# Third and fourth x chunks loaded by one transposing DMA, and the final wait moved from SyncE to ScalarE

## The chip, the core and the metric

The kernel runs on one core of a Trainium2 chip. The metric is the time of one execution on the device in microseconds (us); lower is better. A profile is one further execution, recorded by the hardware profiler; it gives a span (first to last instruction of the program) and a record of every instruction, DMA packet and semaphore update.

The core's engines are named PE (TensorE, matmuls), DVE (VectorE), ACT (ScalarE), POOL (GpSimd) and SP (SyncE). SP computes nothing here: its program issues nearly all DMAs and waits for what they need.

## The reference

Two blocks read the same x (2048 tokens, width 512) and are mixed by a gate for each token:

```python
x = A_x
g = _sigmoid((x * gate_w).sum(-1, keepdims=True))
a = _A_ref(x, A_wqkv, A_w_phi, A_wo)   # linear attention, 32 heads of 16:
                                       # softmax feature maps of +-q and +-k, kv sums, o = num / den, o @ wo
b = _B_ref(x, B_w1, B_w2)              # relu(x @ w1) @ w2, inner width 1376
return g * a + (1 - g) * b
```

All inputs and the output are bf16; the output is 2048 x 512.

## The kernel before

Tokens lie in 16 tiles of 128 (index `m`) and 4 chunks of 512 (index `c`; chunk `c` holds tiles 4c to 4c+3). The matmuls need x with its features on the partitions. That is `XT`, of 128 partitions, 4 feature blocks and 2048 tokens. Chunk 0 is read plainly and transposed on PE, so that work can start early. Chunks 1 to 3 come through transposing DMAs (line 174), each with a semaphore of its own: `x1`, `x2`, `x3`. `xready(c)` (line 202) gives the events that a reader of chunk `c` waits for.

The order of work on each engine is written out by hand. A small planner (`_Plan`) holds one list per engine: `op` adds an instruction, `dma` a DMA on an engine's queue (its semaphore rises by 16 when the data has landed), `wait` a bare wait. `emit` turns each list into that engine's program and leaves out waits that the engine has already made.

SP's list runs in this order. First come the loads: x chunk 0 (line 150), W1 (154 and 164), the small `WPS` (166), `WV` (168), the transposed q and k weights (171) and x chunks 1 to 3 (174). The transposes inside the core follow as their data is made: the ragged last block of the hidden layer for each chunk (279), `PHQ` for each tile (377, after POOL's line 372), and later `OT` for each tile (454). W2 and WO are loaded in between (562 to 567), and each finished tile of the output is stored by line 491.

PE's list has three stages. In the first, chunk 0's hidden units are made from `slab` (line 501). In the second, the loop of line 553 runs for each tile the q and k projection (`atile`, 309), the kv sums of the tile three back (`kv`, 406), the v projection of the tile three ahead (`vtile`, 384) and some hidden units of the chunks (`hunit`, 255; the list `mid` says which). Chunk 2 is first read by `vtile(8)` in the pass `m` = 5, chunk 3 by `vtile(12)` in the pass `m` = 9. In the third stage each tile is finished: numerator and denominator (`nd`, 438), the second dense layer (`finB`, 463), the output projection (`finA`, 472), and the mix on DVE (`comb`, 486).

The last tile's `comb` is cut into 384 and 128 columns. The first cut is stored from SP's queue and the second from ACT's (lines 600 and 601). Both, and the stores of tiles 13 and 14, count on one semaphore, `fin`. Line 602 lets SP wait until all of `fin` has arrived. That bare wait is the last instruction of SP's program; the last of ACT's is its store.

Of the kernel before, what the change touches and what calls it, by code (L numbers as in the profile page):

```python
# [57 lines left out]
def bass_gated_mix__linear_kernel_hedgehog__dense_activation_relu__prompt_kernel(  # L58
# [11 lines left out]
    x2 = A_x.rearrange("b s d -> (b s) d")  # L70
# [6 lines left out]
    NT = S // P  # L77
    NDT = D // P
    NCH = S // 512
# [14 lines left out]
    with ExitStack() as es:  # L94
        E = es.enter_context
        XT = E(nc.sbuf_tensor("XT", [P, NDT, S], BF16))
# [42 lines left out]
        p = _Plan(["sp", "pool", "act", "dve", "pe"])  # L139
# [22 lines left out]
        for t in range(1, NDT):  # L162
            loadw1(t, 0, 8 * P)
        p.dma("sp", lambda e: e.dma_start(
            out=W1[:, :, 8 * P:DFF], in_=B_w1[:, 8 * P:DFF].rearrange("(j p) n -> p j n", p=P)), "w1r", ev="w1r")
        p.dma("sp", lambda e: e.dma_start(
            out=WPS[:, :, :], in_=A_w_phi.rearrange("(g hl) r c -> (hl r) g c", g=NDT)), "wps", ev="wps")
        p.dma("sp", lambda e: e.dma_start(
            out=WV[:, :, :], in_=A_wqkv[:, 2 * D:3 * D].rearrange("(j p) n -> p j n", p=P)), "wv", ev="wv")
        for i in range(2):  # L170
            p.dma("sp", lambda e, i=i: e.dma_start_transpose(
                out=WQKT[:, 4 * i:4 * i + 4, :], in_=A_wqkv[:, i * D:(i + 1) * D]), f"wqk{i}", ev=f"wqk{i}")
        for c in range(1, NCH):
            p.dma("sp", lambda e, c=c: e.dma_start_transpose(
                out=XT[:, :, c * 512:(c + 1) * 512], in_=x2[c * 512:(c + 1) * 512, :]), f"x{c}", ev=f"x{c}")

        p.op("pool", lambda e: e.iota(COLI[:, :], [[1, P]], channel_multiplier=0))
        p.op("pool", lambda e: e.iota(ROWI[:, :], [[0, P]], channel_multiplier=1), ev="iota0")
# [21 lines left out]
             after=["r64"], ev="m32")  # L200

        def xready(c):
            return ["xa0", "xa1", "xa2", "xb0", "xb1", "xb3"] if c == 0 else [f"x{c}"]

        def gatecol(bank):
            gp = PS[:, bank, :].bitcast(BF16)[:, 0:NDT]
# [45 lines left out]
        def hunit(c, kt, eng="act", bank=None):  # L252
            bank = nextbank() if bank is None else bank
            for t in range(NDT):
                p.op("pe", lambda e, t=t: e.matmul(  # L255
                    PS[:, bank, :], W1[:, t, kt * P:(kt + 1) * P], XT[:, t, c * 512:(c + 1) * 512],
                    start=(t == 0), stop=(t == NDT - 1)),
                    after=(xready(c) + w1all + free[bank] if t == 0 else ()),
                    ev=(f"h{c}_{kt}" if t == NDT - 1 else None))
            relu(c, kt, bank, eng)  # L260

        def rest(c):
            bank = nextbank()
            for i in range(4):
                for s in range(NDT):
                    t0 = c * 512 + i * P
                    p.op("pe", lambda e, i=i, s=s, t0=t0: e.matmul(  # L267
                        PS[:, bank, i * P:i * P + NR + 1], XT[:, s, t0:t0 + P], W1[:, s, KU * P:DFF + 1],
                        start=(i == 0 and s == 0), stop=(s == NDT - 1), skip_group_check=True),
                        after=(xready(c) + w1all + ["gw"] + free[bank] if i == 0 and s == 0 else ()),  # L270
                        ev=(f"h{c}_r" if i == 3 and s == NDT - 1 else None))
            src = PS[:, bank, :].rearrange("p (i n) -> p i n", i=4)
            b = c % 2
            p.op("act", lambda e: e.activation(HR[:, b, :, 0:NR], src[:, :, 0:NR], ACT.Relu),
                 after=[f"h{c}_r"] + ([f"hr{c - 2}"] if c >= 2 else []), ev=f"rr{c}")
            p.op("act", lambda e: e.activation(
                EG[:, 4 * c:4 * c + 4].unsqueeze(2), src[:, :, NR:NR + 1], ACT.Exp, scale=-1.0), ev=f"eg{c}")
            free[bank] = [f"eg{c}"]
            p.dma("sp", lambda e: e.dma_start_transpose(
                out=HT[:, KU, c * 512:(c + 1) * 512].rearrange("p (i t) -> p i t", i=4),  # L280
                in_=HR[:, b, :, :].rearrange("p i n -> p (i n)")), f"hr{c}", after=[f"rr{c}", f"hz{b}"], ev=f"hr{c}")
# [20 lines left out]
        def atile(m):  # L302
            b = m % NB
            first = xready(m // 4) + ([f"pc{i}" for i in range(8)] if m == 0 else [])
            order = [(dt, w) for dt in range(NDT) for w in range(2)]
            if m - 1 in split:
# [175 lines left out]
        def comb(m, cs=slice(0, 512), tag="", eng="sp"):  # L482
            ob = m % 3
            bank = fbank[(m, tag)]
            n = cs.stop - cs.start
            p.op("dve", lambda e: e.scalar_tensor_tensor(  # L486
                out=OSB[:, ob, cs], in0=PS[:, bank, 0:n], scalar=OMG[:, m:m + 1],
                in1=TFA[:, m % 2, cs], op0=ALU.mult, op1=ALU.add),
                after=[f"fb{m}{tag}", f"ta{m}"] + ([f"out{m - 3}"] if m >= 3 else []), ev=f"cb{m}{tag}")
            free[bank] = [f"cb{m}{tag}"]  # L490
            p.dma(eng, lambda e: e.dma_start(out=orow(m)[:, cs], in_=OSB[:, ob, cs]),
                  f"out{ob}" if m < NT - 3 else "fin", after=[f"cb{m}{tag}"], ev=f"out{m}{tag}")
# [60 lines left out]
        for m in range(NT):  # L553
# [7 lines left out]
            if m == 3:  # L561
                p.dma("sp", lambda e: e.dma_start(
                    out=W2[:, 0:KU, :], in_=B_w2[0:KU * P, :].rearrange("(j p) n -> p j n", p=P)), "w2", ev="w20")
                p.dma("sp", lambda e: e.dma_start(out=W2[0:NR, KU, :], in_=B_w2[KU * P:DFF, :]), "w2", ev="w2")
            if m == 5:
                p.dma("sp", lambda e: e.dma_start(
                    out=WO[:, :, :], in_=A_wo.rearrange("(j p) n -> p j n", p=P)), "wo", ev="wo")
# [31 lines left out]
            finB(m, (4, 3)[i], cs, "ab"[i])  # L599
        for i, cs in enumerate(cuts):  # L600
            comb(m, cs, "ab"[i], ("sp", "act")[i])
        p.wait("sp", [f"out{NT - 1}b"])

        sems = {}
        for name in p.count:
# [31 lines left out]
```

## Time and profile before

| what | value |
|---|---|
| median of 4 runs | 148.77 us (148.73, 148.76, 148.77, 149.47) |
| the profiled execution's own time | 149.25 us |
| its span | 147.9 us |
| granted PE clock | 1.00 throughout |
| busy in the span | PE 143.1, DVE 92.7, ACT 72.2, POOL 52.1 us |
| instructions of the program: SP, POOL, ACT, DVE | 80, 90, 156, 203 records |
| DMA moved | 16.12 MB; queue q1 is SP's, q10 is ACT's |
| instruction loads in the span | q8: 8 packets, 0.13 MB; q14: 5 packets, 0.04 MB |

The span does not hold all of the execution: 149.25 - 147.89 = 1.36 us lie outside of it. The profile's records of semaphore updates go on after the program's last instruction: the engines meet there on a semaphore numbered 2, clear the other semaphores, and meet once more, until 149.365 us on the span's clock.

Instructions of an engine are listed with their line of the kernel. "SPq" and "ACTq" are the engines' DMA-issuing instructions. A wait is listed as who waited, for whom, the time in total, the count and the longest.

### The profile page before, as it was taken

Reading aid. Unit: us, or ns where it says so; the run is one execution under the profiler, and the core shown is the slowest. Engines: PE = TensorE matmul, PEld = TensorE weight load, DVE = VectorE, ACT = ScalarE, POOL = GpSimd, SP = SyncE. Lnnn points to the kernel's source line nnn. Section 1 sums busy time; section 2 is a strip of 40 time slices with the busy share of each in tenths; the row PEclk is TensorE's granted clock in tenths of the full one; section 3 lists DMA queues with packets and bytes.
Section 4 is the critical chain, followed back from the end, with each engine's and each line's share of the span. In section 5 each row is a group of like instructions: output and inputs, shape, how many; then the busy total and the mean of one; then the engine's idle time right before and its main releaser. Section 6 shows DMA issues by size and latency. Waiting matters only on the chain.

```text
span 147.9 us, 2515 instructions
## 1 busy us (share of the span) xinstructions
PE 143.1 (97%) x961; PEld 73.2 (50%) x978; DVE 92.7 (63%) x156; ACT 72.2 (49%) x124; POOL 52.1 (35%) x62
## 2 busy tenths in 40 slices
PE   7999999999999999999999999999999999999992
PEld 2544744444455545545645555554444444444451
DVE  2327946777688878678698968664555555554242
ACT  3307627887778778887878861122111111111150
POOL 2022001788768678688869810200000000000000
PEclk9999999999999999999999999999999999999999
DMA  4999993033339985334634432355322223233312
GB/s 153 267 284 202 227 208 78 0 71 71 75 86 308 169 212 75 71 71 106 78 71 87 90 71 40 79 108 132 76 71 71 71 71 75 71 78 92 80 42 71
DMA packets 45173, 16.12 MB, mean 109 GB/s; under 512 B 39304, under 2 KB 44520, under 8 KB 45160
## 3 DMA queue, kind: packets, MB, share of 16 engines
q1 hardware_dynamic: 45008, 15.92, 48.1%
q8 instruction: 8, 0.13, 0.4%
q10 hardware_dynamic: 152, 0.03, 0.1%
q14 instruction: 5, 0.04, 0.1%
HBM read 4.41 MB, written 2.10 MB: 44 GB/s over the span
## 4 chain that ended last, share of the span: by engine, by line
PE 96%; DVE 1%; issue 1%; ACT 0%
PE PS L463 25%; PE PS L255 19%; PE PS L309 18%; PE PS L472 9%; PE PS L384 9%; PE PS L501 5%; PE PS L438 3%; PE PS L406 3%; PE PS L213 2%; PE PS L267 2%; PE PS L289 1%; PE PS L219 1%; DVE WQK L486 1%; DVE XT L229 0%; ACT XT L232 0%
## 5 line engine op out<-in xcount | busy, mean ns | idle before, releaser
L463 PE MATMUL PS<-W,HT 128*128 128x512 bf16 (+4 forms) x181 | 40.0, 366 | 0.3
L328 ACT ACTIVATE EB<-PS 128x480 bf16<-128x480 f32 (+1 forms) x44 | 30.1, 757 | 15.9 <-PE PS L309 15.9
L352 POOL TENSOR_TENSOR EB<-EB,SC 128x1024 bf16<-128x1024 bf16 x15 | 28.9, 1928 | 24.5 <-DVE SC L350 24.5
L477 ACT ACTIVATE TFA<-PS,GT 128x512 bf16<-128x512 f32 x16 | 11.0, 687 | 42.7 <-PE PS L472 36.6
L255 PE MATMUL PS<-XT,W 128*128 128x512 bf16 x124 | 30.0, 379 | 0.2
L309 PE MATMUL PS<-WQK,XT 128*128 128x480 bf16 x128 | 28.5, 366 | 0.0
L486 DVE SCALAR_TENSOR_TENSOR WQK<-PS,OMG,TFA 128x512 bf16<-128x512 f32 (+2 forms) x17 | 12.2, 719 | 23.6 <-ACT TFA L477 22.4
L348 DVE TENSOR_REDUCE ZB<-EB 128x64 f32<-128x1024 bf16 x15 | 18.3, 1220 | 13.9 <-ACT EB L328 13.9
L463 PEld LDWEIGHTS PS<-W,HT 128*128 128x128 bf16 (+1 forms) x187 | 17.0, 98 | 17.4
L241 ACT ACTIVATE HT<-PS 128x512 bf16<-128x512 f32 x35 | 20.3, 616 | 7.3 <-PE PS L501 5.4
L309 PEld LDWEIGHTS PS<-WQK,XT 128*128 128x128 bf16 x128 | 12.5, 98 | 13.8
L363 DVE TENSOR_REDUCE ZB<-EB 128x64 f32<-128x1024 bf16 x16 | 18.6, 1164 | 0.0
L255 PEld LDWEIGHTS PS<-XT,W 128*128 128x128 bf16 x128 | 12.0, 98 | 13.2
L372 POOL TENSOR_TENSOR EB<-EB,SC 128x512 bf16<-128x512 bf16 x16 | 16.9, 1055 | 1.2
L472 PE MATMUL PS<-WO,OT 128*128 128x512 bf16 x63 | 16.0, 378 | 0.1
L384 PE MATMUL PS<-WV,XT 128*128 128x512 bf16 x59 | 15.3, 379 | 0.3
L448 DVE TENSOR_TENSOR WQK<-PS,RDEN 128x512 bf16<-128x512 f32 x16 | 11.1, 691 | 0.5
L472 PEld LDWEIGHTS PS<-WO,OT 128*128 128x128 bf16 x64 | 6.1, 97 | 7.2
L350 DVE RECIPROCAL SC<-ZB 128x64 f32<-128x64 f32 x16 | 8.9, 553 | 0.5
L394 ACT ACTIVATE VS<-PS 128x512 bf16<-128x512 f32 x13 | 7.9, 611 | 0.0
L384 PEld LDWEIGHTS PS<-WV,XT 128*128 128x128 bf16 x64 | 5.5, 97 | 4.9
L501 PE MATMUL PS<-XT,W 128*128 128x512 bf16 x31 | 7.6, 391 | 0.3
(55 smaller groups left out, 87.7 us busy)
## 6 DMA issues: line engine op xcount, KB each, us to landing
out_dram<-WQK SPq DMA_DIRECT2D x15, 128.0 KB, 1.7
W<-in_B_w_dram SPq DMA_DIRECT2D x1, 1280.0 KB, 7.4
W<-in_B_w_dram SPq DMA_DIRECT2D x3, 256.0 KB, 4.6
OT<-in_A_x_dram SPq DMA_DIRECT2D x2, 256.0 KB, 2.9
WV<-in_A_wqkv_dram SPq DMA_DIRECT2D x1, 512.0 KB, 6.4
WO<-in_A_wo_dram SPq DMA_DIRECT2D x1, 512.0 KB, 4.5
W<-in_B_w_dram SPq DMA_DIRECT2D x1, 352.0 KB, 5.9
W<-in_B_w_dram SPq DMA_DIRECT2D x2, 128.0 KB, 3.3
```

Source lines behind the costliest of these rows:

```text
L241: p.op("act", lambda e: e.activation(dst, src, ACT.Relu), after=[f"h{c}_{kt}"], ev=ev)
L255: p.op("pe", lambda e, t=t: e.matmul(PS[:, bank, :], W1[:, t, kt * P:(kt + 1) * P], XT[:, t, c * 512:(c + 1) * 512], start=(t == 0), stop= ...
L309: p.op("pe", lambda e, dt=dt, which=which: e.matmul(PS[:, which, 0:DE], XT[:, dt, m * P:(m + 1) * P], WQK[:, which, dt * DE:(dt + 1) * DE] ...
L328: p.op("act", lambda e: e.activation(dst, s_, ACT.Exp, scale=scale), after=[f"qk{m}"] + busy, ev=ev)
L348: p.op("dve", lambda e: e.tensor_reduce(zk, ek, AX.X, ALU.add), after=[emk, f"cst{b}"], ev=f"zk{m}")
L352: p.op("pool" if m < NT - 1 else "dve", lambda e: e.tensor_tensor(EB[:, b, 3, :].rearrange("p (g f) -> p g f", f=DH), EB[:, b, 2, :].rearr ...
L363: p.op("dve", lambda e: e.tensor_reduce(ZB[:, b, 0:64].rearrange("p (h s) -> p h s", s=2), bass.AP(tensor=EB, offset=base, ap=[[EBS, P], [ ...
L372: p.op("pool", lambda e: e.tensor_tensor(EB[:, b, 0, :].rearrange("p (h s f) -> p h s f", h=H, s=2)[:, :, 1, :], EB[:, b, 1, :].rearrange( ...
L384: p.op("pe", lambda e, dt=dt: e.matmul(PS[:, bank, :], XT[:, dt, m * P:(m + 1) * P], WV[:, dt, :], start=(dt == 0), stop=(dt == NDT - 1)), ...
L463: p.op("pe", lambda e, kt=kt, M=M: e.matmul(PS[:, bank, 0:n], HT[0:M, kt, m * P:(m + 1) * P], W2[0:M, kt, cs], start=(kt == 0), stop=(kt = ...
L472: p.op("pe", lambda e, t=t: e.matmul(PS[:, bank, :], OT[:, t, m * P:(m + 1) * P], WO[:, t, :], start=(t == 0), stop=(t == NDT - 1)), after ...
L501: p.op("pe", lambda e, u=u: e.matmul(PS[:, UB[u], :], W1[:, t, u * P:(u + 1) * P], XT[:, t, 0:512], start=(t == 0), stop=(t == NDT - 1)), ...
```

## The change

The third and fourth chunk (tokens 1024 to 2047) are loaded by one transposing DMA in place of two, with one semaphore, `x2`. Readers of chunk 3 wait for `x2` in place of `x3`. The bare wait at the end is given to ACT. SP's program goes from 80 to 78 recorded instructions, ACT's from 156 to 157.

```diff
-        for c in range(1, NCH):
-            p.dma("sp", lambda e, c=c: e.dma_start_transpose(
-                out=XT[:, :, c * 512:(c + 1) * 512], in_=x2[c * 512:(c + 1) * 512, :]), f"x{c}", ev=f"x{c}")
+        for c0, c1 in ((1, 2), (2, NCH)):
+            p.dma("sp", lambda e, t0=c0 * 512, t1=c1 * 512: e.dma_start_transpose(
+                out=XT[:, :, t0:t1], in_=x2[t0:t1, :]), f"x{c0}", ev=f"x{c0}")
...
         def xready(c):
-            return ["xa0", "xa1", "xa2", "xb0", "xb1", "xb3"] if c == 0 else [f"x{c}"]
+            return ["xa0", "xa1", "xa2", "xb0", "xb1", "xb3"] if c == 0 else [f"x{min(c, 2)}"]
...
             comb(m, cs, "ab"[i], ("sp", "act")[i])
-        p.wait("sp", [f"out{NT - 1}b"])
+        p.wait("act", [f"out{NT - 1}b"])
```

## The prediction

> **What bounds the kernel now.** I read the page first, then the chain of waits, then the end of the timeline, then the DMA queues in the last microseconds, because the change touches SP alone and SP computes nothing.
>
> ```profile
> PE 143.1 (97%) x961; PEld 73.2 (50%) x978; DVE 92.7 (63%) x156; ACT 72.2 (49%) x124; POOL 52.1 (35%) x62
> PE 96%; DVE 1%; issue 1%; ACT 0%
> ```
>
> PE is busy for 143.1 of 147.9 us and holds 96% of the chain that ends last. Between its first and last matmul its gaps over 20 ns come to 1.1 us in all. A change on SP can therefore pay or cost in two places only: where a load comes so late that PE stands still, or in the stretch after the last matmul. The chain and the timeline of that stretch:
>
> ```profile
> 142.58 1.80 PE PS L463 x11
> 144.38 0.03 issue
> 144.41 0.97 DVE WQK L486 x2
> ```
>
> ```profile
> 143.31 2.08 SPq L491 DMA_DIRECT2D out_dram<-WQK  x2
> 144.41 0.97 DVE L486 SCALAR_TENSOR_TENSOR WQK<-PS,OMG,TFA 128x384 bf16<-128x384 f32 x2 [1.13 <-PE PS L463]
> 145.41 0.38 ACTq L491 DMA_DIRECT2D out_dram<-WQK  x1
> ```
>
> ```profile
> SPq L51 <- DMA out_dram<-WQK: 2.5, 1, 2.5
> ```
>
> The last output is combined by 145.38, ACT issues its store from 145.41 to 145.79, and SP's bare wait (its line is the helper's, L51) lasts 2.5 us, until 147.89. That is the end of the span. Why 2.5 us? The queues in the window from 146.6 to the end:
>
> ```profile
> q14 instruction: 1, 0.01, 1.5%
> q10 hardware_dynamic: 9, 0.00, 0.7%
> ```
>
> The last store went out as 128 packets of 256 B, with one 4-byte packet on each of the 16 DMA engines that counts it. Fifteen engines are through by 146.57. In this window the sixteenth still has its 8 data packets and its counting packet to send: the packet records show them from 147.00 to 147.11, straight behind one 8,192-byte instruction load that ran there from 146.69 to 147.00. The semaphore records agree: 15 of the last store's 16 counts have arrived by 147.00, the sixteenth comes at 147.85. In this execution an instruction load cost up to 147.85 - 147.00 = 0.85 us.
>
> **Whose load it is.** Queue q14 has five such loads in the span, at 48.50, 51.16, 70.39, 133.60 and 146.69. POOL's at 70.39 starts 1.06 us after the instruction at 69.32, its 68th, behind which it falls; those at 48.50 and 133.60 lie 127 of DVE's records apart, so one load seems to hold about that many instructions. A load is thus about 1.1 to 1.3 us behind its cause, which puts the cause of the last at 145.4 to 145.6. SP finishes issuing at 145.39 and enters its bare wait, its 80th and last recorded instruction. I take the load for SP's; that is an inference from times.
>
> The Trainium skill (Runtime: NRT & Kernel Launch, section "Instruction fetch mechanics") says that an engine refills its instruction memory in blocks of 256 instructions and that crossing a block is mostly hidden. The trace has blocks of 8,192 B on q14, half of that, and the last one in the only place where nothing hides it. By the page, shortening SP's program would be worth nothing; by the row it could be worth 0.85 us.
>
> **The parts of the change.**
>
> The joined load. SP's queue around it:
>
> ```profile
> 14.06 7.14 SPq L174 DMA_TRANSPOSE XT<-in_A_x_dram  x3
> 21.32 1.20 SPq L279 DMA_TRANSPOSE HT<-HR  x1
> 28.64 1.23 SPq L377 DMA_TRANSPOSE PHQ<-EB  x1
> ```
>
> The three issues take 2.11, 2.91 and 2.04 us; the first (chunk 1) stays as it is. The trace shows no transpose of 1024 rows, so I bound it. From below: as long as one of the two, 2.04 us. From above: twice the slowest transposing load of 512 rows, 2 x 5.45 = 10.9 us (line 171). I take 2.91 + 2.04 = 4.95 us, because the bytes are the same and SP's issue keeps step with the packets there. The issue begins at 16.21, so SP is free between 18.3 and 27.1, at 21.2 by my value. Queued behind it is line 279 with 1.20 us, which lands in a buffer that is read only after 89 us, and then line 377, which waits for POOL until 28.64 anyhow; even the upper bound leaves 27.1 + 1.2 = 28.3. The data: `x2` arrived at 21.49 and `x3` at 23.41. Together they come by 23.4, or by 27.1 plus some 2 us at the upper bound. The first reader is `vtile(8)`:
>
> ```profile
> 43.34 0.86 PE PS L384 x4
> ```
>
> So PE's work on other chunks covers it by 43.3 - 23.4 = 19.9 us. Without that cover every microsecond of delay would be one on PE. Term: 0.
>
> The joined semaphore and the one wait fewer in readers: nothing. PE's wait for `x3` at `vtile(12)` is replaced by one that it has already made.
>
> The wait on ACT. Behind ACT's store stands nothing of the program, so nothing is held up in it. After the program the engines meet on semaphore 2. Its updates come at 145.166; then 146.055, 146.094, 146.138; then 148.058, 148.101, 148.139, 148.174, 148.220. The group at 146.06 begins 0.26 us after ACT's last issue ends (145.794), the group at 148.06 begins 0.17 us after SP's wait ends (147.888). I read this as a chain of turns in which ACT starts three and SP comes after them. Before, from the wait's end to the chain's end: 0.17 + 0.162 = 0.332 us. After, the wait ends on ACT, and ACT's three turns come late as well: 0.17 (SP's reaction) to 0.26 (ACT's) to ACT's update, then 0.039 + 0.044 to the third, then the five that follow when nobody is late, which the second meeting shows at 149.125 to 149.365: 0.024 + 0.097 + 0.038 + 0.035 + 0.046 = 0.240. That is 0.49 to 0.58 us, which is 0.16 to 0.25 more than before. Bound below: 0, if what is timed does not hold this meeting or ACT is not in that turn; a gain is excluded, since all that followed SP's turn before follows ACT's turn now, with two turns more. I take 0.21, the middle. Term: +0.21.
>
> The shorter program. Bounds: -0.85 us (the load leaves the last store's way) to +0.85 (a load that was clear of it gets into it). Two instructions fewer put the block's edge two instructions later, into what SP runs after its program. But SP now has no wait there: it goes on at 145.39, and what SP does from its wait's end to its turn on semaphore 2 took 0.17 us before. So the load is caused within 0.17 us of where it was, and arrives by 146.9 at the latest, still among the last store's packets. I take the value nearest to that row: 0.
>
> **Sum.** 0 + 0.21 + 0 = +0.21 us. For the profiled execution: 149.25 + 0.21 = 149.46, with the span still near 147.9. It lies 0.48 above the median of the runs; on the median, 148.77 + 0.21 = **148.98 us**. Its own range is 148.8 to 149.15 (0.16 to 0.25 and the scatter of the runs of some 0.1).
>
> **Rivals.**
>
> First, the load gets out of the way: the edge falls behind SP's turn on semaphore 2, where SP stands until ACT has come. For it: a stretch of a few instructions decides, and two is of that size. Against it: SP reached its turn in 0.17 us, which leaves room for several. The time: -0.85 + 0.21 = -0.64, 148.13; and if the meeting costs nothing, -0.85, 147.92.
>
> Second, on the slower side: the load newly gets into the way. The timed runs lie 0.48 below the profiled one, and one of four (149.47) 0.7 above the others, as if most of them were free of the collision that the profile caught. A load moved by up to 0.17 us, against a store issued at 145.41 on ACT, may then hit one DMA engine in every run: 0.85 + 0.21 = +1.06, 149.83. It decides from a delay of 0.53 us on, as 0.74 (0.5% of the median) - 0.21. Against it: SP's instant hardly moves.
>
> Third, the joined load does not do the work of two at the same pace and arrives after 43.3. For it: no such shape is in the trace. Against it: it would have to take 27 us from its issue at 16.2, against some 7 (16.2 to 23.4) for the two. At 45 us it would cost 1.7: 150.7.
>
> **Chances.** The forecast 0.48, the first rival 0.30 (half of it at 147.92), the second 0.17, the third 0.05. What a measurement of this kernel can tell from no change is about 0.5%, 0.74 us. Faster by more: the half of the first rival below 148.03, 0.15. Slower by more, above 149.51: the second and third, 0.22. Within: 0.63. The range of 148.1 to 149.85 leaves out the faster half of the first rival and the third, 0.20.
>
> **What would show it.** In the changed profile: one transposing issue of about 5 us at line 174 that lands near 23.4, and PE's gaps as before. The last wait on ACT, ending near 147.9, with one q14 load between 146.6 and 146.9 and a count of `fin` that lags behind the others by more than 0.5 us. Semaphore 2's second, third and fourth update after that wait in place of at 146.06. I am wrong if that q14 load is gone or later than 147 (first rival), if the semaphore's chain is not longer, or if PE stands before line 384 at 43 us.

## The result, and the profile after

The changed kernel takes 148.45 us (median of 44 runs, the fastest 147.83); the kernel before, measured beside it, 148.97. The ratio is 0.9964, 95% interval 0.9955 to 0.9974: 0.36% faster. That is inside the 0.5% that the prediction called no change, but the interval is clear of 1, and the forecast of 148.98 had the sign wrong.

The profiled execution after took 148.10 us with a span of 146.64, against 149.25 and 147.89 before. Three windows in each trace say where the 1.25 us of span went: from the start to the first matmul of line 255, from there to the end of the last matmul, and from the end of the last combination on DVE to the end of the span. The first columns are the window and its length; the rest is busy time (with the number of instructions) of PE, PE's weight loads, DVE, ACT and POOL, then granted clock, DMA share and GB/s. Before:

```profile
0.00:12.94 12.94, 11.89 (x54) 5.47 (x56) 4.69 (x24) 3.95 (x7) 2.81 (x15) 1.00 0.88 233
12.94:144.99 132.05, 131.21 (x908) 67.78 (x922) 87.63 (x132) 68.28 (x118) 49.24 (x47) 1.00 0.45 98
145.38:147.89 2.51, 0.00 (x0) 0.00 (x0) 0.00 (x0) 0.00 (x0) 0.00 (x0) 1.00 0.20 56
```

After:

```profile
0.00:12.63 12.63, 11.40 (x55) 5.39 (x56) 4.70 (x24) 3.96 (x7) 2.81 (x15) 1.00 0.89 241
12.63:144.67 132.04, 131.19 (x908) 67.83 (x922) 87.63 (x132) 68.28 (x118) 49.26 (x47) 1.00 0.47 98
145.06:146.64 1.58, 0.00 (x0) 0.00 (x0) 0.00 (x1) 0.00 (x0) 0.00 (x0) 1.00 0.32 88
```

The long middle is the same to 0.01 us. The first window is 0.31 shorter; there PE waits for the first W1 and x loads, and the same window takes 12.4 to 13.4 us in the profiles of the other kernels here, whatever their edit: scatter. The last window is 0.93 us shorter, though no engine computes in it. It holds the last store.

How long is that store on its way? From ACT's issue to the sixteenth count it took 2.44 us before and 1.51 us after. The profile's list of DMA issues shows the same (what is written and read, queue, count, KB, median us from issue to landing), before and after, each in a window around the end:

```profile
out_dram<-WQK ACTq DMA_DIRECT2D x1, 32.0 KB, 2.4
```

```profile
out_dram<-WQK SPq DMA_DIRECT2D x1, 96.0 KB, 1.6
out_dram<-WQK ACTq DMA_DIRECT2D x1, 32.0 KB, 1.5
```

The instruction load on q14 has not gone. It starts at 146.337, which is 1.24 us behind ACT's issue, where it was 1.28 behind before. But the last store's packets are all through by 146.268. The queues of the changed kernel from 146.28 to the end of the span:

```profile
DMA packets 1, 0.01 MB, mean 23 GB/s; under 512 B 0, under 2 KB 0, under 8 KB 0
## 3 DMA queue, kind: packets, MB, share of 16 engines
q14 instruction: 1, 0.01, 8.9%
```

Only the load itself is left. Before, nine packets of the store stood behind it: one DMA engine's share, eight data packets and the counting one. The packet records do not name the DMA engine; that the load and the nine share one is read from their times, since the first of the nine starts within 0.01 us of the load's end.

The joined load and SP's queue after:

```profile
13.65 7.17 SPq L174 DMA_TRANSPOSE XT<-in_A_x_dram  x2
20.94 1.20 SPq L279 DMA_TRANSPOSE HT<-HR  x1
28.33 13.86 SPq L377 DMA_TRANSPOSE PHQ<-EB  x4
```

Two issues take 7.17 us where three took 7.14; the joined one takes 5.12 and lands 7.3 us after its start, at 23.0, with the first reader at 43.03.

### The profile page after: what moved, and what is told of

Its sections match the earlier page's. It is cut to its first block, busy times and chain, and to the rows that moved or that the text cites. A ratio compares the mean times of both kernels' runs of the same rounds, so it can differ in the third digit from the quotient of the medians.

```text
span 146.6 us, 2513 instructions
## 1 busy us (share of the span) xinstructions
PE 142.6 (97%) x961; PEld 73.2 (50%) x978; DVE 92.7 (63%) x156; ACT 72.2 (49%) x124; POOL 52.1 (36%) x62
## 4 chain that ended last, share of the span: by engine, by line
PE 96%; DVE 1%; issue 1%; ACT 0%
PE PS L463 25%; PE PS L255 19%; PE PS L309 18%; PE PS L472 9%; PE PS L384 9%; PE PS L501 5%; PE PS L438 3%; PE PS L406 3%; PE PS L213 2%; PE PS L267 2%; PE PS L289 1%; PE PS L219 1%; DVE WQK L486 1%; DVE XT L229 0%; ACT XT L232 0%
## 5 line engine op out<-in xcount | busy, mean ns | idle before, releaser
L255 PE MATMUL PS<-XT,W 128*128 128x512 bf16 x124 | 30.0, 379 | 0.2
L438 PEld LDWEIGHTS PS<-KVNZ,PHQ 128*128 128x128 bf16 x128 | 6.1, 97 | 3.6
```

The costliest lines, as they stand in the source:

```text
L255: p.op("pe", lambda e, t=t: e.matmul(PS[:, bank, :], W1[:, t, kt * P:(kt + 1) * P], XT[:, t, c * 512:(c + 1) * 512], start=(t == 0), stop= ...
```

## The experiments

Theory A was that what counts is the place of the edge of SP's instruction block: the instruction at which SP enters a new block causes a load about 1.1 to 1.3 us later, and the load costs time only if it stands ahead of the last store's packets on its DMA engine. Theory B: the wait on ACT pays by itself. Theory C: the joined load pays by itself. A further rival was that a shorter program of SP pays as such.

By theory A the edge lies at SP's 80th recorded instruction. In the kernel before that is the final wait. Instructions that SP runs behind its program are not recorded, so where the edge lies among them is counted, not seen.

### Each half of the change alone

Only the wait moved (79 recorded instructions on SP):

```diff
-        p.wait("sp", [f"out{NT - 1}b"])
+        p.wait("act", [f"out{NT - 1}b"])
```

> The kernel before with only the final wait moved to ScalarE; the loads stay three. SyncE's program has 79 recorded instructions, one fewer. Theory A (instruction load: the time goes with where the edge of SyncE's instruction block falls, and whether the load that it causes stands in the way of the last store): the edge falls on the first instruction after the program, which SyncE reaches at once, so the load is caused some 20 to 150 ns later than in the kernel before; if that small shift is what counts, it gains most of what the change gained: 148.3 to 148.6 us where the kernel before has 148.97, with 0.1 to 0.15 us more between the span's end and the end of the execution. Theory B (the wait itself: ScalarE notices the end sooner, or SyncE's waiting delays the store): the whole gain of 0.5 us or more. Theory C (the joined load is what pays): no gain, 149.0 to 149.1.

Measured: 149.08 us, ratio 1.0002 (0.9980 to 1.0024): no gain. Theory B falls. So does theory A's own expectation of most of the gain: in the profile the load starts at 146.161, which is 1.06 us behind ACT's issue and so earlier than in the kernel before, not later as expected, and the store is hit as before. From 146.3 on:

```profile
DMA packets 9, 0.00 MB, mean 2 GB/s; under 512 B 9, under 2 KB 9, under 8 KB 9
## 3 DMA queue, kind: packets, MB, share of 16 engines
q10 hardware_dynamic: 9, 0.00, 0.8%
```

These are again one DMA engine's share of the last store, and they start at the load's end. The sixteenth count comes at 147.478, the fifteenth at 146.628.

Only the load joined (79 on SP, the last of them the wait):

```diff
-        p.wait("act", [f"out{NT - 1}b"])
+        p.wait("sp", [f"out{NT - 1}b"])
```

(against the changed kernel)

> The kernel before with only the third and fourth chunks joined; SyncE keeps the final wait, as its 79th and last recorded instruction. Theory A: the edge falls on the first instruction behind the final wait, so the load is caused only when the last store has landed; no q14 packet stands between 145.5 us and the end of the span, and the last store's sixteenth count follows the others closely. Then 148.1 to 148.4 us (ratio 0.994 to 0.996), better than the change, since the longer meeting of the engines behind ScalarE's wait is not paid. Theory B: no gain, 148.9 to 149.1. Theory C: the whole gain, 148.4.

Measured: 148.79 us, ratio 0.9982 (0.9962 to 1.0003), less than theory A said and not clear of no change. The profile shows both halves of the reason. The store is free, and between 144.5 us and the end of the span there is no instruction load; it comes after the span, at 147.696:

```profile
q1 hardware_dynamic: 144, 0.10, 16.8%
q10 hardware_dynamic: 144, 0.03, 8.0%
```

The span is shorter: its median is 146.9 us against 147.6. But crossing the edge costs SP time of its own. From the end of SP's wait (146.388) to its update of semaphore 2 (147.043) it took 0.66 us, where it took 0.17 before, and the others stand there for SP. The time outside of the span is 1.87 us in the median against 1.33. A joined load that paid by itself (theory C) has no place in this: PE's middle stage was unchanged.

### More instructions on SP

One recorded instruction more than before (81), added where SP is idle at 22 to 28 us; several waits share one recorded instruction:

```diff
+        for ev in ("iota0", "iota"):
+            p.wait("sp", [ev])
         for m in range(NT):
             atile(m)
```

> The kernel before with one recorded instruction MORE on SyncE (81): two waits on long-finished work of GpSimd are added while SyncE is idle at some 22 to 28 us. Nothing else changes. Theory A: the edge moves to the store of the last tile's first cut, at which SyncE stands from some 143.7 us on, so the load comes near 145.0 us, ahead of the last two stores; the last store is free: 148.1 to 148.5 us, faster than the kernel before although the program is longer. That a shorter program of SyncE pays by itself: 149.0 or more. Theories B and C: no change.

Measured: 148.06 us, ratio 0.9928 (0.9900 to 0.9956). A longer program is faster than both kernels. The load starts at 144.571, 0.4 us earlier than expected. The packets of tile 14's store are through by 144.50, and the last store's begin only at 146.14. The final wait lasts 1.6 us where it lasted 2.5 (from the same edit's second run, below):

```profile
SPq L491 <- DVE WQK L486: 5.2, 3, 2.9
SPq L51 <- DMA out_dram<-WQK: 1.6, 1, 1.6
```

Three more (83), by the same lines with eleven events in the list:

> As the run with one more, but with three recorded instructions more on SyncE (83). Theory A: the edge moves to the store of tile 13, at which SyncE stands from some 139.5 us on, so the load comes near 140.8 us, where PE's work hides it: the same gain as with one more, 148.1 to 148.5 us. That a shorter program pays by itself: 149.0 or more.

Measured: 148.31 us, ratio 0.9944 (0.9923 to 0.9965). The load starts at 140.585 and touches nothing that PE waits for. Why this kernel's median is 0.25 us above that with one more is not shown; the two intervals overlap. Both runs contradict that a shorter program pays as such.

### More and fewer, with the change in place

The changed kernel with one recorded instruction more (79), by the two added waits of the 81-instruction kernel:

> The changed kernel with one recorded instruction more on SyncE (79 in place of 78): two added waits on long-finished work while SyncE is idle. Joined load and wait on ScalarE stay. Theory A (where the edge of SyncE's instruction block falls decides): the edge is back where it was in the run with the wait on ScalarE alone, so the load stands in the way of the last store again in most executions: 148.9 to 149.1 us, the gain gone. If the joined load or the moved wait paid in themselves: 148.45 as in the changed kernel.

Measured: 149.20 us, ratio 1.0002 (0.9981 to 1.0022). This one instruction takes the whole gain away; joined load and moved wait are still there. The profile, from 147.1 us on:

```profile
DMA packets 10, 0.01 MB, mean 8 GB/s; under 512 B 9, under 2 KB 9, under 8 KB 9
## 3 DMA queue, kind: packets, MB, share of 16 engines
q14 instruction: 1, 0.01, 1.5%
q10 hardware_dynamic: 9, 0.00, 0.7%
```

It is the picture of the kernel before: one load and, within 0.01 us of its end, nine packets of the last store.

The changed kernel with two more (80), by four events in the list:

> The changed kernel with two recorded instructions more on SyncE (80). Theory A: the edge falls on the store of the last tile's first cut, so the load comes near 144.6 us and the last store is free in every execution; what remains is the longer meeting behind ScalarE's wait, 0.15 us more than in the run with one instruction added to the kernel before (148.06): 148.1 to 148.35 us. If fewer instructions paid: slower than the changed kernel's 148.45.

Measured: 148.12 us, ratio 0.9938 (0.9915 to 0.9962), as theory A had it. The load starts at 144.307.

The kernel before with SP's bare waits for the constants left out (76):

```diff
-                f"tq{b}", after=[f"pq{m}", f"cst{b}"] + (["pm7"] if m == 12 else []), ev=f"tq{m}")
+                f"tq{b}", after=[f"pq{m}"] + (["pm7"] if m == 12 else []), ev=f"tq{m}")
```

> The kernel before with SyncE's four bare waits for the constants' memsets left out (they are implied by GpSimd's results, which come after them): 76 recorded instructions, the final wait on SyncE as the last. Theory A: the edge falls on the fourth instruction behind the final wait, so the load is caused after the last store has landed; no q14 packet between 145.5 us and the span's end; span 146.4 to 147.0. In the joined-load run the crossing itself held SyncE 0.5 us on its way to the engines' meeting (0.66 us from its wait to its update of semaphore 2, in place of 0.17); if the fourth instruction is still ahead of that update the time is as there, 148.7 to 148.9; if it is behind it, SyncE's own clearing hides it: 148.0 to 148.3.

Measured: 148.31 us, ratio 0.9954 (0.9934 to 0.9974). The store is free (its last count 1.54 us behind ACT's issue), and SP reaches semaphore 2 in 0.13 us: the edge lies behind that update. The load comes at 148.430. The time outside of the span is 1.54 us in the median against 1.33 before; no record shows what the 0.21 are.

The same line in the changed kernel (74):

> The changed kernel without the same bare waits: 74 recorded instructions on SyncE. Theory A: the edge falls on the sixth instruction behind SyncE's last issue. If SyncE reaches it before it has to stand for ScalarE, the load still comes among the last store's packets, later by some 0.1 to 0.2 us than in the changed kernel, and hits it more seldom: 148.2 to 148.45. If SyncE stands before it, the load comes after the end: no q14 packet between 145 us and the span's end, 148.1 to 148.35. A gain that grows with each instruction taken away (148.2 or less for four fewer, and e7 faster than 148.4 for the same reason) would speak for program length itself.

Measured: 148.61 us, ratio 0.9974 (0.9956 to 0.9991). The expected time was too low. The store is free (1.50 us) and the span short (146.75 in the median), but the time outside of the span is 1.82 us against 1.45 in the changed kernel. The load starts at 148.285, after the engines' last recorded meeting at 148.264, and the crossing is paid behind it. That the crossing causes those 0.37 us is my reading; no record shows SP there.

### The changed kernel and the best version side by side

> The changed kernel once more, beside the version with one instruction more. Open so far: its spans (median 147.0 us) lie between those of kernels whose last store is free (146.65 to 146.75) and those whose store is hit (147.6 to 147.75). If its load misses the last store in every execution, the span comes out at 146.7 to 146.8 and the time at 148.2; if it hits in some, the span is near 147.0 and the time near 148.45 again, with single executions above 147.4.

> The kernel before with one recorded instruction more on SyncE (81), once more, beside the changed kernel: 148.05 to 148.25 us, 0.2 to 0.4 us faster than the changed kernel on the same chip. If the first result was luck: level with the changed kernel at 148.45.

Neither kernel has a new edit here. Measured on one chip, where the kernel before took 149.01 us with a median span of 147.7: the changed kernel 148.28 us, ratio 0.9958 (0.9942 to 0.9974); one instruction more 148.05, ratio 0.9938 (0.9921 to 0.9954). The medians are 0.23 us apart, as expected, though the two intervals overlap. The spans, 146.8 and 146.7 in the median, are nearly level; the rest is time outside of the span, 1.46 against 1.32. No span of the changed kernel is above 147.3 here, which is nearer to a load that misses in every execution than to one that hits in some.

> One more profile of the changed kernel, to see whether its load now stands in the way of the last store: a sixteenth count more than 0.5 us behind the others if it does, within 0.1 us if it does not.

> As the look before: a hit would show as a sixteenth count more than 0.5 us behind the others. If the changed kernel is hit in about a third of its executions, one of the three new profiles should show it.

In both the store is free: the last count 1.53 and 1.52 us behind ACT's issue, the last two counts 0.003 and 0.017 us apart. So it is in the changed kernel's other two profiles. Four free profiles do not rule out a hit in a third of the executions: by chance alone that would happen one time in five.

All edges in one table. "Where the edge falls" is counted by theory A. "Span" and "outside" are medians over the timed runs, in us; the changed kernel's row is of the first 44 runs, that of the kernel before of the runs beside the first experiments:

| kernel | SP records, who waits last | where the edge falls | last count behind ACT's issue | span | outside | time |
|---|---|---|---|---|---|---|
| before | 80, SP | the final wait | 2.44 | 147.6 | 1.33 | 148.95 |
| wait moved alone | 79, ACT | 1st behind SP's last issue | 2.38 | 147.6 | 1.47 | 149.08 |
| changed + 1 | 79, ACT | 1st behind SP's last issue | 2.45 | 147.75 | 1.44 | 149.20 |
| changed | 78, ACT | 2nd behind SP's last issue | 1.51 | 147.0 | 1.45 | 148.45 |
| changed - 4 | 74, ACT | 6th; after the meeting | 1.50 | 146.75 | 1.82 | 148.61 |
| load joined alone | 79, SP | 1st behind the final wait | 1.51 | 146.9 | 1.87 | 148.79 |
| before - 4 | 76, SP | 4th behind the final wait | 1.54 | 146.7 | 1.54 | 148.31 |
| before + 1 | 81, SP | store of tile 15's first cut | 1.54 | 146.75 | 1.33 | 148.06 |
| changed + 2 | 80, ACT | the same store | 1.52 | 146.65 | 1.49 | 148.12 |
| before + 3 | 83, SP | store of tile 13 | 1.54 | 147.0 | 1.31 | 148.31 |

All three profiles with the load in the way have 2.38 to 2.45 us, all eleven others 1.50 to 1.59. The price of being hit is 0.8 to 0.95 us in the profile and 0.6 to 1.1 in the median spans. The place of the load follows the count as well: in 13 of the 14 profiles it starts 1.08 to 1.33 us after the last instruction that SP is recorded to finish ahead of the edge, while its place moves from 140.6 to 148.4 us. The fourteenth, the changed kernel less four, has no such record: there the edge falls, by the count, behind SP's turn in the engines' meeting.

The table also holds pairs in which the change is made with the edge in the same place or with the same outcome for the store. Before + 1 and changed + 2, both with the edge at the store of tile 15's first cut, take 148.06 and 148.12 us. Before and changed + 1, both hit, take 148.95 and 149.20. So the joined load and the moved wait in themselves gain nothing.

## Why the prediction was wrong, point by point

**What bounds the kernel: right.** But for scatter at the start, the whole effect lay behind the last matmul; PE's middle stage took 132.04 to 132.05 us in every profile.

**Whose load it is: right.** Taking one SP instruction away or adding one moved that load and no other of q14's five: the others stay within 1 us of their places in every profile.

**The joined load, 0: right.** The bound from both sides was not needed; 5.12 us for 1024 rows is the sum of the two (4.95) within 4%, and nobody waited.

**The wait on ACT, +0.21: right in sign, too large.** The time outside of the span rose from 1.33 to 1.45 us, +0.12. In the profile the way from the wait's end to the end of the meeting went from 0.332 to 0.430 us. The mis-sized term is ACT's reaction, which I took at 0.17 to 0.26 and which is 0.108 (146.644 to 146.752); the seven gaps behind it summed to 0.322, as worked out.

**The shorter program, 0: here it failed.** The prediction said that the load, being caused within 0.17 us of where it was, arrives "still among the last store's packets" and took 0 as nearest. The instant was right: 1.24 us behind ACT's issue in place of 1.28. What does not follow is that it is still in the way. Already in the kernel before, the other fifteen shares of the store were through by 146.58, ahead of the load's 146.69; the packets that it was among were only the nine that it held up itself. The two edges next to each other differ by one instruction and by the whole effect: one behind the last issue is hit as before, two behind it is free. The term was about -0.6 us in the medians of the first measurement (span 147.6 to 147.0), -0.9 in those of the second (147.7 to 146.8) and -0.93 in the two profiles. With +0.12 for the wait on ACT, the first gives -0.48 us, where -0.52 was measured.

I had treated the load and the store as overlapping intervals, where being close in time means being in the way. I read them now as two entrants to one DMA engine, of which the first makes the other wait; the two outcomes are shown, what picks between them is not. A term with two values and nothing between should have been carried as two cases. None of the three signs by which the prediction would be wrong came. What told was that the sixteenth count no longer lagged by over 0.5 us, and that lag had been named for the case that the prediction was right. The first rival was this case; it asked for the load to come after the meeting, which was more than was needed, and gave 148.13 from an undiminished 0.85.

**The second rival** rested on the timed runs being mostly free of the collision. They were not: the spans of the kernel before start at 147.2 us, where those of the free kernels start at 146.4 to 146.6, and their median lies 0.6 to 1.0 above. The 0.48 us between the profiled run and the median, from which the rival argued, is no more than the first 13 us scatter by.

## What to carry to other kernels

When a profile shows a store at the end with one DMA engine's counts far behind the others, look for an instruction load on that stretch, and count the instructions of the engine that just ran out of work. Then move the block's edge by adding or taking away an instruction, best to where the compute engine still hides it: here one added instruction was worth 0.6 to 0.7%, more than the change, and a shorter program was worth nothing as such. A difference of one instruction between two kernels can so be mistaken for the value of an edit; compare both kernels with the edge in the same place before believing it.

## What the runs showed of the hardware that I had not expected

Where SP crossed the edge of its instruction block, it was held up itself, by about 0.5 us: with only the load joined, it took 0.66 us from its wait to its next update with the edge there, and 0.13 to 0.17 in the kernels without. That is one profile; the 12 timed runs of that kernel agree, with 0.54 us more outside of the span than the kernel before. SP did not stand for the load's data, which began to move 0.65 us after that update. It costs time there because the other engines stand for SP.

The Trainium skill (Runtime: NRT & Kernel Launch, section "Instruction fetch mechanics") calls the cost of crossing a block mostly hidden. The traces agree for the four of the five q14 loads in the span of the kernel before that fall into PE's middle stage, which is 132.04 to 132.05 us long in every profile; for the last one they do not.

The start stamp of the load does not tell who was first. It is 1.06, 1.28 and 1.28 us behind ACT's issue where the store was hit, and 1.23 to 1.30 where it was free, in four profiles of the changed kernel. In these four it lies 0.06 to 0.14 us behind the last packet of the store. In the kernel before, the sixteenth share was held back before the load's data began to move: the other fifteen were through at 146.58, the load's data began at 146.69, and the share followed at 147.00. What orders the two stays open; so does whether the changed kernel is hit in a few of its executions.
